# Attention keys loaded once, local scores from row tiles, and weight loads reordered in an attention and mixture-of-experts kernel

## The chip, the core and the metric

The kernel runs on one NeuronCore of a Trainium2 chip. The metric is the device time of one execution in microseconds (us); lower is better. Each engine of the core (TensorE or PE, VectorE or DVE, ScalarE or ACT, GpSimd or POOL, and SyncE or SP, which issues most transfers here) works through its own instructions in a fixed order and waits for the others on semaphores.

## What is computed

Three stages follow each other. The first is attention over 4 batches, 8 heads, 576 positions and 64 channels, the sum of a pooled branch (queries, keys and values averaged over groups of 4 positions) and a local branch (each query sees keys closer than 4 positions):

```
q_d, k_d, v_d = means of q, k, v over 4 neighbouring positions
out_up    = repeat(softmax(scale * q_d @ k_d.T) @ v_d, 4)
mask      = |i - j| < 4
out_local = softmax(where(mask, scale * q @ k.T, -1e9)) @ v
x = out_up + out_local                       # 2304 tokens x 512
```

The second is `h = ((x @ w1) * (x @ w2)) @ w3 @ w_out`, with 64-bit weights that the kernel turns to fp32 itself. The third sends each token to the one expert (of 8) with the largest gate logit: `out = gate * sigmoid(output gate) * relu(h @ w1[e]) @ w2[e]`.

## The kernel before

**Stages.** The kernel first turns the eight pieces of `w_out` from 64-bit to fp32 (`gate_step`, three DVE operations for each piece in `f64_bits`, L127 to L129), then sixteen pieces of `w3` (`w3_part`) and multiplies `w3` with `w_out` on PE (`wc_half`). Behind that come six groups of 384 tokens: `g1_step` (x with w1 and w2) and `g2_step` (with the product of w3 and w_out), both from the helper `mm3` (L398 to L400). Then come the experts. Up to about 104 us of the profiled execution the `w3` stage runs, from there to about 371 us the token groups into which attention is woven, and behind that the experts.

**Attention units.** Attention is cut into 16 units of two heads (`NU`). Each unit has five steps: `a_T` (pooled sums of queries and keys), `a_S1` (scores), `a_S2` (normalizing), `a_V1` (transposes) and `a_V2` (weighted values). The list `side` holds all steps in a staggered order. `step()` takes the next ones out at fixed places of the weight and token loops (tables `GSTEP`, `W3STEP`, `G1STEP`, `G2STEP`), and after a step it issues loads for the next unit. Within that, the framework's list scheduler sets the final order on each engine by its own model of times, so the order of the program text is not that of the engines.

**Keys.** A unit's keys come twice: whole into `kc` (L157, one buffer), which `a_T` sums in fours (`kd`, L185), and head by head into `kz` (L164, one buffer). `kz` has both heads side by side in the free dimension and zeros where a head's row half doesn't belong, so that one matmul with all 128 rows gives both heads' scores. The local scores are 24 fp32 matmuls of 32 queries by 64 columns (two heads of 32 keys), each in one of four 32-column strips of the array:

```python
nc.tensor.matmul(sl[32 * j:32 * j + 32, b], qT[:, 24 * g:24 * g + 32], kz[:, :, 24 * g:24 * g + 32],
                 start=True, stop=True, tile_position=(0, 32 * j))          # L196
```

An fp32 matmul stands in the trace as two records, so a unit has 48 on L196. Three matmuls follow for the pooled scores (`sd`, L208, six records); both groups have the same high priority, and the scheduler may mix them. All their PSUM tiles, and those of `a_V1` and `a_V2`, come from one ring of three banks (`psa`, tag `at`).

**Behind the scores.** DVE adds the mask (L200) and takes the maximum (L201); POOL subtracts it (L202). For the pooled scores DVE takes the maximum (`md`, L211) and scales it (L212), and ACT takes the exponentials with it as bias (L216). POOL adds up pooled values (`v4`, called `v` in the trace, L235 and L236, loaded at L168). The windows of values for the local branch are `vw` (L173).

**Loads.** All these loads, those of the weights (`f64_load`, L119) and the stores of g2_step go through SP's one queue in order. A load whose buffer is still in use makes everything behind it wait. The loads of `w1` and `w2` (`ahead()`) go into other buffers than those of `w3`, and nothing orders the two; `w_gate` and `w_ogate` are loaded in strips of 8 floats (L886, L887).

## Time and profile before

| | us |
|---|---|
| three runs: median (lowest to highest) | 742.13 (741.83 to 745.91) |
| the profiled execution: its own time | 743.41 |
| the profiled execution: span of its instructions | 741.7 |
| PE busy in the span | 706.0 |
| DVE, POOL, ACT busy in the span | 437.9, 324.5, 280.3 |

The mean granted TensorE clock is 0.986 of full speed. Shares of busy time are means over stages that are bound by different things, so the stages have to be looked at one by one: the first 30 us, the rest of the `w3` stage up to 104 us, the token groups with attention up to 371 us, and the experts.

### The profile page before, as it was taken

Reading aid. Unit: us, or ns where it says so; the run is one execution under the profiler, and the core shown is the slowest. Engines: PE = TensorE matmul, PEld = TensorE weight load, DVE = VectorE, ACT = ScalarE, POOL = GpSimd, SP = SyncE. Lnnn points to the kernel's source line nnn. Section 1 sums busy time; section 2 is a strip of 40 time slices with the busy share of each in tenths; the row PEclk is TensorE's granted clock in tenths of the full one; section 3 lists DMA queues with packets and bytes.
Section 4 is the critical chain, followed back from the end, with each engine's and each line's share of the span. In section 5 each row is a group of like instructions: output and inputs, shape, how many; then the busy total and the mean of one; then the engine's idle time right before and its main releaser. Section 6 shows DMA issues by size and latency. Waiting matters only on the chain.

```text
span 741.7 us, 14714 instructions
## 1 busy us (share of the span) xinstructions
PE 706.0 (95%) x5710; PEld 671.9 (91%) x5711; DVE 437.9 (59%) x940; ACT 280.3 (38%) x624; POOL 324.5 (44%) x306
## 2 busy tenths in 40 slices
PE   5788999999999999999999999989999999999995
PEld 3677889989989998998999999979999999999994
DVE  8979899872565437254342342575756756766730
ACT  3436356541254135034212221244454444544610
POOL 6845586950263146123012020155564755854611
PEclk9899999999999999999999999989999999999999
DMA  8998657611153133110100100566444645545301
GB/s 326 316 243 246 186 142 246 212 57 57 28 161 111 43 92 96 57 45 24 57 30 1 43 0 30 171 224 219 170 154 149 218 166 203 184 162 221 115 24 40
DMA packets 38265, 97.72 MB, mean 132 GB/s; under 512 B 6019, under 2 KB 12931, under 8 KB 38193
## 3 DMA queue, kind: packets, MB, share of 16 engines
q1 hardware_dynamic: 34768, 86.82, 36.4%
q0 software_dynamic: 3424, 9.93, 3.7%
q8 instruction: 46, 0.75, 0.4%
q14 instruction: 27, 0.21, 0.1%
HBM read 84.93 MB, written 12.29 MB: 131 GB/s over the span
## 4 chain that ended last, share of the span: by engine, by line
PE 76%; DMA 7%; POOL 6%; issue 6%; DVE 4%; ACT 1%; SPq 0%; POOLq 0%; DVEq 0%; ACTq 0%
PE g L398 22%; PE g L399 21%; PE g L400 21%; DMA v<-in_v_dram 3%; PE at L268 2%; DMA vw<-in_vw_dram 2%; PE at L208 1%; PE at L196 1%; PE tr L694 1%; PE at L264 1%; PE tr L787 1%; PE g L330 1%; PE at L252 1%; POOL out_dram L777 1%; DMA early<-in_moe_w_dram 1%
## 5 line engine op out<-in xcount | busy, mean ns | idle before, releaser
L398 PE MATMUL g<-xh,W 128*128 128x384 f32 x384 | 131.0, 341 | 0.6 <-DVE a L427 0.5
L400 PE MATMUL g<-xh,W 128*128 128x384 f32 x384 | 129.8, 338 | 0.7 <-POOL W L377 0.6
L399 PE MATMUL g<-xl,W 128*128 128x384 f32 x384 | 129.3, 337 | 0.0
L721 DVE TENSOR_TENSOR W<-raw,W 128x1024 fp32r<-128x1024 f32 x32 | 87.9, 2781 | 32.6 <-ACT W L719 23.5
L721 POOL TENSOR_TENSOR W<-raw,W 128x1024 fp32r<-128x1024 f32 x29 | 82.9, 2880 | 36.9 <-ACT W L719 36.9
L398 PE MATMUL g<-xT,W 128*128 128x288 f32 (+6 forms) x256 | 82.0, 320 | 1.0 <-ACT xT L698 1.0
L431 POOL TENSOR_TENSOR h<-a,h 128x384 fp32r<-128x384 f32 x30 | 30.8, 1028 | 118.4 <-ACT h L429 118.4
L399 PE MATMUL g<-xT,W 128*128 128x288 f32 (+6 forms) x256 | 80.1, 313 | 0.0
L400 PE MATMUL g<-xT,W 128*128 128x288 f32 (+6 forms) x256 | 79.8, 312 | 0.0
L398 PEld LDWEIGHTS g<-xh,W 128*128 128x128 f32 x384 | 72.2, 188 | 2.1 <-DVE a L427 0.9
L400 PEld LDWEIGHTS g<-xh,W 128*128 128x128 f32 x384 | 72.1, 188 | 2.0 <-POOL W L377 1.8
L399 PEld LDWEIGHTS g<-xl,W 128*128 128x128 f32 x384 | 72.2, 188 | 0.3 <-issue 0.2
L398 PE MATMUL g<-h,W 128*128 128x288 f32 (+5 forms) x224 | 69.9, 312 | 0.0
L399 PE MATMUL g<-wc,h 128*128 128x272 f32 (+1 forms) x240 | 68.2, 285 | 0.0
L398 PE MATMUL g<-wc,h 128*128 128x272 f32 (+1 forms) x240 | 68.2, 285 | 0.0
L399 PE MATMUL g<-h,W 128*128 128x288 f32 (+5 forms) x224 | 68.0, 303 | 0.0
L400 PE MATMUL g<-h,W 128*128 128x288 f32 (+5 forms) x224 | 68.0, 303 | 0.0
L400 PE MATMUL g<-wc,h 128*128 128x272 f32 (+1 forms) x240 | 67.8, 285 | 0.0
L719 ACT CAST W<-raw 128x1024 fp32r<-128x1024 f32 x61 | 60.0, 1046 | 8.3 <-DMA raw<-in_moe_w_dram 4.4
L427 DVE TENSOR_TENSOR a<-g,a 128x384 f32<-128x384 f32 x48 | 26.6, 554 | 61.9 <-PE g L400 49.6
L747 ACT ACTIVATE h<-g 128x288 fp32r<-128x288 f32 (+6 forms) x64 | 27.9, 437 | 78.1 <-PE g L400 74.2
L777 POOL DMA_INDIRECT out_dram<-orow,b_si x24 | 23.5, 978 | 62.9 <-DVE orow L776 59.3
(255 smaller groups left out, 1716.3 us busy)
## 6 DMA issues: line engine op xcount, KB each, us to landing
raw<-in_moe_w_dram SPq DMA_DIRECT2D x61, 512.0 KB, 3.5
f64w<-in_moe_w_dram SPq DMA_DIRECT2D x16, 512.0 KB, 8.5
f<-in_moe_w_dram SPq DMA_DIRECT2D x16, 512.0 KB, 4.7
vw<-in_vw_dram SPq DMA_DIRECT2D x16, 384.0 KB, 4.9
kc<-in_k_dram SPq DMA_DIRECT2D x16, 288.0 KB, 8.8
qT<-in_q_dram SPq DMA_DIRECT2D x16, 288.0 KB, 3.2
kz<-in_k_dram SPq DMA_DIRECT2D x32, 144.0 KB, 4.1
v<-in_v_dram SPq DMA_DIRECT2D x16, 288.0 KB
```

The source lines that it names most:

```text
L196: nc.tensor.matmul(sl[32 * j:32 * j + 32, b], qT[:, 24 * g:24 * g + 32], kz[:, :, 24 * g:24 * g + 32], start=True, stop=True, tile_positio ...
L208: nc.tensor.matmul(sd[:, qb], qf[:, 96 * qb:96 * qb + 96], d["kd"], start=True, stop=True)
L268: nc.tensor.matmul(xl[c // 3][64 * h:64 * h + 64, 96 * (c % 3):96 * (c % 3) + 96], vw[:, c, D * h:D * h + D], bd[:, 2 * c + h, :], start=T ...
L398: nc.tensor.matmul(ps, whi, xhi, start=first, stop=False)
L399: nc.tensor.matmul(ps, whi, xlo, start=False, stop=False)
L400: return nc.tensor.matmul(ps, wlo, xhi, start=False, stop=last)
L427: nc.vector.tensor_tensor(a, pp[1][:, 0:G], a, op=ALU.mult)
L431: eng.tensor_tensor(lo, a, hi.bitcast(F32), op=ALU.subtract)
L719: nc.scalar.copy(out=hi, in_=t)
L721: ins = eng.tensor_tensor(lo, t, hi.bitcast(F32), op=ALU.subtract)
L747: return nc.scalar.activation(out=t[:, 0, 0:C], in_=ps[:, 0:C], func=AF.Relu), nc.vector.scalar_tensor_tensor(t[:, 1, 0:C], ps[:, 0:C], 0. ...
L777: ins = nc.gpsimd.indirect_dma_start(out=out, out_offset=bass.IndirectOffsetOnAxis(ap=rt["si"][0:n, r, b:b + 1], axis=0), in_=t[0:n], in_o ...
```

## The change

The keys come once, into one of two buffers `kT` (128 rows: both heads' channels). The local scores are 48 matmuls of 32 queries by 32 keys over 64 rows each, head 0 in the upper and head 1 in the lower half of the array's rows, and each head has a PSUM bank of its own. The mask is added per head. The pooled scores are issued behind the local ones (`tc.issue_after`), the scaling of their maximum goes to ACT, the first loads of `w1` and `w2` are issued behind the last load of `w3`, and the two gate matrices are laid out by the host so that each row is one piece of 128 bytes.

```diff
@@ -101,6 +101,7 @@
 
 
     staged = {}
+    f64_last = [None]
 
     def pieces(m, n):
         return (slice(0, 256), slice(256, 512)) if (m, n) == ("o", 0) else (slice(0, 512),)
@@ -116,7 +117,7 @@
             t = mt([P, 512], I64, "f64", tag=f"W{3 + 4 * m}") if n % 2 and n < 6 else mt([P, 512], I64, "f64", bufs=2)
             src = (w1, w2)[m][n]
         for c in pieces(m, n):
-            nc.sync.dma_start(out=t[:, c], in_=src[:, c])
+            f64_last[0] = nc.sync.dma_start(out=t[:, c], in_=src[:, c])
         staged[m, n] = t
 
     def f64_bits(t, dst):
@@ -138,11 +139,11 @@
     def at(shape, dt, name, bufs=1):
         return att.tile(shape, dt, name=name, tag=name, bufs=bufs)
 
-    kz = at([P, 2, 584], F32, "kz")
+    kTs = [at([P, 584], F32, f"kT{i}") for i in range(2)]
     qTs = [at([P, 584], F32, f"qT{i}") for i in range(2)]
     bd = at([P, 12, 96], F32, "bd")
     qz = at([P, 2, 144], F32, "qz")
-    for t in (kz, *qTs, bd, qz):
+    for t in (*qTs, *kTs, bd, qz):
         nc.gpsimd.memset(t, 0.0)
     st = {}
 
@@ -152,16 +153,10 @@
 
     def a_load(u):
         d = st.setdefault(u, {})
-        qT = qTs[u % 2]
-        kc = at([P, S], F32, "kc")
-        nc.sync.dma_start(out=kc, in_=k[u])
+        qT, kT = qTs[u % 2], kTs[u % 2]
+        nc.sync.dma_start(out=kT[:, 3:3 + S], in_=k[u])
         nc.sync.dma_start(out=qT[:, 0:S], in_=q[u])
-        d.update(kc=kc, qT=qT)
-
-    def a_loadk(u):
-        for h in range(2):
-            c = slice(64 * h, 64 * h + 64)
-            nc.sync.dma_start(out=kz[c, h, 3:3 + S], in_=k[u, c])
+        d.update(kT=kT, qT=qT)
 
     def a_loadd(u):
         v4 = at([72, 2, 4, 2 * D], F32, "v4")
@@ -182,34 +177,37 @@
             c = slice(64 * h, 64 * h + 64)
             nc.gpsimd.tensor_tensor(qz[c, h], hs[c, :, 0], hs[c, :, 1], op=ALU.add)
         dn = at([P, 144], F32, "kd")
-        nc.vector.tensor_reduce(out=dn, in_=d["kc"].rearrange("p (n t) -> p n t", t=4), axis=AX.X, op=ALU.add)
+        nc.vector.tensor_reduce(out=dn, in_=d["kT"][:, 3:3 + S].rearrange("p (n t) -> p n t", t=4), axis=AX.X, op=ALU.add)
         d["kd"] = dn
 
     def a_S1(u):
         d = st[u]
-        qT = d["qT"]
-        ps = psa.tile([P, 512], F32, name="at", tag="at")
-        sl = ps[:, 0:384].rearrange("p (b h k) -> p b h k", b=6, h=2)
+        qT, kT = d["qT"], d["kT"]
+
+        sl = [psa.tile([P, 512], F32, name="at", tag="at")[:, 0:192].rearrange("p (b k) -> p b k", b=6) for _ in range(2)]
         with burst():
             for g in range(24):
                 b, j = divmod(g, 4)
-                nc.tensor.matmul(sl[32 * j:32 * j + 32, b], qT[:, 24 * g:24 * g + 32], kz[:, :, 24 * g:24 * g + 32],
-                                 start=True, stop=True, tile_position=(0, 32 * j))
+                for h in range(2):
+                    c = slice(64 * h, 64 * h + 64)
+                    end = nc.tensor.matmul(sl[h][32 * j:32 * j + 32, b], qT[c, 24 * g:24 * g + 32], kT[c, 24 * g:24 * g + 32],
+                                     start=True, stop=True, tile_position=(64 * h, 32 * j))
         sm = at([P, 6, 2, 32], F32, "sm", bufs=2)
         mx = at([P, 6, 2], F32, "mx")
-        nc.vector.tensor_tensor(sm, sl, mask.unsqueeze(2).to_broadcast([P, 6, 2, 32]), op=ALU.add)
+        for h in range(2):
+            nc.vector.tensor_tensor(sm[:, :, h], sl[h], mask, op=ALU.add)
         nc.vector.tensor_reduce(out=mx, in_=sm, axis=AX.X, op=ALU.max)
         nc.gpsimd.tensor_tensor(sm, sm, mx.unsqueeze(3).to_broadcast([P, 6, 2, 32]), op=ALU.subtract)
         ps = psa.tile([P, 512], F32, name="at", tag="at")
         sd = ps[0:96, 0:432].rearrange("p (q k) -> p q k", q=3)
         qf = qz.rearrange("p h n -> p (h n)")
-        with burst():
+        with burst(), tc.issue_after(end.ins):
             for qb in range(3):
                 nc.tensor.matmul(sd[:, qb], qf[:, 96 * qb:96 * qb + 96], d["kd"], start=True, stop=True)
         ed = at([96, 3, 144], F32, "ed", bufs=2)
         md = at([96, 3], F32, "md")
         nc.vector.tensor_reduce(out=md, in_=sd, axis=AX.X, op=ALU.max)
-        nc.vector.tensor_scalar(md, md, -1.0 / 128, None, op0=ALU.mult)
+        nc.scalar.mul(md, md, -1.0 / 128)
         zd = at([96, 3], F32, "zd", bufs=2)
         nc.scalar.activation(out=sm, in_=sm, func=AF.Exp, scale=0.125)
         for qb in range(3):
@@ -303,8 +301,6 @@
                 if fn is a_T and u + 1 < NU:
                     a_load(u + 1)
                 if fn is a_S1:
-                    if u + 1 < NU:
-                        a_loadk(u + 1)
                     a_loadd(u)
 
 
@@ -883,14 +879,13 @@
     nc.vector.memset(wg, 0.0)
     for n in range(KF):
         if n == 1:
-            nc.sync.dma_start(out=wg[:, :, 0:E], in_=w_gate.rearrange("(k p) e -> p k e", p=P))
-            nc.sync.dma_start(out=wg[:, :, E:2 * E], in_=w_ogate.rearrange("(k p) e -> p k e", p=P))
+            nc.sync.dma_start(out=wg[:, :, 0:E], in_=w_gate.rearrange("p (k e) -> p k e", e=E))
+            nc.sync.dma_start(out=wg[:, :, E:2 * E], in_=w_ogate.rearrange("p (k e) -> p k e", e=E))
         f64_load("o", n)
     for n in range(4):
         f64_load("3", n)
         if n == 1:
             a_load(0)
-            a_loadk(0)
     gps = ps2.tile([P, 512], F32, name="g2", tag="g2")
     for f in range(KF):
         gate_step(f, gps, staged.pop(("o", f)))
@@ -913,7 +908,8 @@
     wf3 = mt([P, 3, 512], F32, "wf3", tag="xl")
     for i in range(KF):
         if i == KF - 2:
-            ahead()
+            with tc.issue_after(f64_last[0].ins):
+                ahead()
         w3T[i] = [mt([P, KF, P], F32R, "w3T", tag=f"W{12 + 2 * (i % 2) + z}") for z in range(2)]
         for hf in range(2):
             n = 2 * i + hf
@@ -1072,6 +1068,8 @@
     a["moe_w3"] = w3.reshape(KF, P, 2, 4, P).transpose(0, 2, 4, 3, 1).reshape(2 * KF, P, 512)
     for n in ("moe_w1", "moe_w2"):
         a[n] = _np.asarray(a[n]).reshape(KD, P, KF, P).transpose(2, 1, 0, 3).reshape(KF, P, 512)
+    for n in ("moe2_w_gate", "moe2_w_output_gate"):
+        a[n] = _np.asarray(a[n]).reshape(KD, P, E).transpose(1, 0, 2).reshape(P, KD * E)
     w = _np.asarray(a["moe2_w1"])
     a["moe2_w1"] = w.reshape(E, KD, P, 4, 256).transpose(0, 3, 2, 1, 4).reshape(E, 4 * P, 1024)
     w = _np.asarray(a["moe2_w2"])
```

**On SP's queue**, from the loads of the first attention unit on. Before (`f64w` is a piece of `w3`, `f_` one of `w1` or `w2`, `v_` the pooled values):

```order
L119 DMA f64w<-in_moe_w_dram 128x512 x2
L158 DMA qT_113<-in_q_dram 128x576
L168 DMA v_380<-in_v_dram 72x1024
L173 DMA vw<-in_vw_dram 128x768
L119 DMA f_1138<-in_moe_w_dram 128x512
L119 DMA f_1140<-in_moe_w_dram 128x512
L119 DMA f_1142<-in_moe_w_dram 128x512
L157 DMA kc<-in_k_dram 128x576
L164 DMA kz<-in_k_dram 64x576 x2
L158 DMA qT_112<-in_q_dram 128x576
L119 DMA f_1144<-in_moe_w_dram 128x512
L119 DMA f64w<-in_moe_w_dram 128x512 x2
```

Of the change:

```order
L120 DMA f64w<-in_moe_w_dram 128x512 x2
L157 DMA kT_112<-in_k_dram 128x576
L158 DMA qT_114<-in_q_dram 128x576
L163 DMA v_402<-in_v_dram 72x1024
L168 DMA vw<-in_vw_dram 128x768
L157 DMA kT_111<-in_k_dram 128x576
L158 DMA qT_113<-in_q_dram 128x576
L120 DMA f64w<-in_moe_w_dram 128x512 x2
```

The four `f_` loads that stood between those of `w3` now stand behind the last of `w3` (twelve of its pieces came after them), and the keys of a unit are one row in place of three.

**On PE**, at the scores of the last attention unit (L196 and L208 before, L193 and L206 now; `g_` is the work of the token groups, L264 the next step of another unit). Before:

```order
L400 MATMUL g_4431<-xh,W_1619 128x384
L196 MATMUL at<-kz,qT_113 32x64 x3
L208 MATMUL at<-kd,qz 96x144
L196 MATMUL at<-kz,qT_113 32x64
L208 MATMUL at<-kd,qz 96x144
L196 MATMUL at<-kz,qT_113 32x64
L208 MATMUL at<-kd,qz 96x144
L196 MATMUL at<-kz,qT_113 32x64 x19
L264 MATMUL at<-pt,vd 64x144 x4
```

Of the change:

```order
L395 MATMUL g_4801<-xl,W_1731 128x384
L396 MATMUL g_4801<-xh,W_1732 128x384
L193 MATMUL at<-kT_112,qT_114 32x32 x48
L206 MATMUL at<-kd,qz 96x144 x3
L394 MATMUL g_4816<-xh,W_1742 128x384
```

The pooled matmuls no longer stand among the local ones, whose number has doubled.

**On PE, at one of six units** in which the two heads now stand apart (L266 is the last step of another unit):

```order
L266 MATMUL at<-bd,vw 64x96 x12
L193 MATMUL at<-kT_111,qT_113 32x32 x24
L394 MATMUL g_3820<-xh,W_1742 128x384
L395 MATMUL g_3820<-xl,W_1742 128x384
L193 MATMUL at<-kT_111,qT_113 32x32 x24
L206 MATMUL at<-kd,qz 96x144 x3
L193 MATMUL at<-kT_112,qT_114 32x32 x48
```

There the first 24 matmuls are those of one head and the second 24 those of the other, with other work between them; behind them the next unit's scores follow at once.

## Rows read from the trace of the kernel before

**Rows 1.** The page's busy time of each engine, its share of the span and instructions.

```profile
PE 706.0 (95%) x5710; PEld 671.9 (91%) x5711; DVE 437.9 (59%) x940; ACT 280.3 (38%) x624; POOL 324.5 (44%) x306
```

**Rows 2.** Busy time by stage: PE, PEld, DVE, ACT, POOL, granted clock, DMA, GB/s.

```profile
0.00:30.00 30.00, 18.35 (x153) 13.32 (x154) 25.86 (x58) 12.61 (x27) 20.93 (x42) 1.00 0.95 327
30.00:104.00 74.00, 65.17 (x738) 58.54 (x739) 65.07 (x141) 33.30 (x96) 44.57 (x52) 0.93 0.77 215
104.00:371.00 267.00, 264.56 (x2392) 249.48 (x2391) 148.99 (x398) 101.55 (x271) 106.99 (x120) 1.00 0.31 94
```

**Rows 3.** What PE waited for from 30 to 104 us: total us, times, longest.

```profile
PE g L398 <- DVE wc L363: 2.3, 1, 2.3
PE g L400 <- POOL w3T L351: 2.2, 1, 2.2
```

**Rows 4.** Two shorter stretches, PE alone: busy, granted clock, DMA, GB/s.

```profile
31.50:38.40 6.90, 5.47 (x30) 0.51 1.04 316
75.90:79.30 3.40, 3.40 (x25) 0.50 0.03 7
```

**Rows 5.** What DVE waited for from 30 to 104 us.

```profile
DVE kd L185 <- DMA kc<-in_k_dram: 3.8, 2, 2.4
DVE sT L243 <- POOL sm L228: 2.6, 1, 2.6
```

**Rows 6.** What POOL waited for from 30 to 104 us.

```profile
POOL v L235 <- DMA v<-in_v_dram: 18.6, 6, 5.3
```

**Rows 7.** What SP's queue waited for from 30 to 104 us.

```profile
SPq L119 <- DVE wf L129: 20.2, 9, 6.0
...
SPq L164 <- PE at L196: 4.2, 2, 3.1
```

**Rows 8.** The page's DMA issues: count, KB each, median us from issue to landing.

```profile
raw<-in_moe_w_dram SPq DMA_DIRECT2D x61, 512.0 KB, 3.5
f64w<-in_moe_w_dram SPq DMA_DIRECT2D x16, 512.0 KB, 8.5
...
kz<-in_k_dram SPq DMA_DIRECT2D x32, 144.0 KB, 4.1
```

**Rows 9.** The first three loads of w1 and w2 on SP's queue: start, us.

```profile
20.45 1.52 SPq L119 DMA_DIRECT2D f<-in_moe_w_dram  x3
```

**Rows 10.** PE at the last unit's scores, in order of time: start, us to the last end.

```profile
337.57 0.31 PE L196 MATMUL at<-kz,qT 128*32 128x64 f32 x6
337.81 0.49 PE L208 MATMUL at<-kd,qz 128*96 128x144 f32 x2
338.23 0.30 PE L196 MATMUL at<-kz,qT 128*32 128x64 f32 x2
...
340.21 0.47 PE L264 MATMUL at<-pt,vd 72*64 72x144 f32 x4
```

**Rows 11.** PE at the scores of a unit that wasn't mixed.

```profile
287.92 0.88 PE L196 MATMUL at<-kz,qT 128*32 128x64 f32 x48
288.72 0.98 PE L208 MATMUL at<-kd,qz 128*96 128x144 f32 x6
289.44 0.43 PE L398 MATMUL g<-xh,W 128*128 128x384 f32 x1
```

**Rows 12.** PE at the first local scores: two windows, of one and of four records.

```profile
22.43 0.24 PE L196 MATMUL at<-kz,qT 128*32 128x64 f32 x1
...
22.43 0.26 PE L196 MATMUL at<-kz,qT 128*32 128x64 f32 x4
```

**Rows 13.** Groups of operations on DVE, 30 to 371 us: busy us, mean ns, idle before.

```profile
L200 DVE TENSOR_TENSOR sm<-at,mask 128x384 f32<-128x384 f32 x15 | 8.1, 540 | 0.2
L212 DVE TENSOR_SCALAR md<-md 96x3 f32<-96x3 f32 x15 | 6.2, 416 | 0.0
```

**Rows 14.** Groups of operations on ACT, the whole span.

```profile
L216 ACT ACTIVATE ed<-at,md 96x144 f32<-96x144 f32 x48 | 17.5, 371 | 20.7 <-DVE md L212 20.6
...
L271 ACT COPY up<-at 128x144 f32<-128x144 f32 x16 | 4.4, 278 | 19.8 <-PE at L268 19.3 <-ACT sm L214 0.2
```

## The prediction

> **What bounds the kernel now.** I first read the page's busy times [rows 1]: PE works 706.0 of 741.7 us, so the end is set by PE wherever PE is full, and by whoever starves it elsewhere. The table by stage tells where that is [rows 2]. From 104 to 371 us PE works 264.56 of 267.00 us at the full clock: there every microsecond of PE work that goes comes off the end, and faster transfers are worth next to nothing. From 30 to 104 us PE and DVE both work 65.1 of 74.0 us, the DMA engines are 0.77 busy, and the clock is 0.93. Before 30 us DVE works 25.86 of 30.00 us and PE 18.35. The experts behind 371 us keep their order and aren't touched.
>
> For the stage from 30 to 104 us I then read the waits. PE's own are single stalls of 2.3 and 2.2 us for DVE and POOL results [rows 3], and in two stretches of 6.90 and 3.40 us its clock is at half, 1.2 in place of 2.4 GHz [rows 4]; both follow stalls of PE. DVE stood 3.8 us for the keys' load and 2.6 us for a POOL product [rows 5]. POOL, which works in order, stood 18.6 us for the pooled values' loads [rows 6]. SP's queue mostly waits for DVE to free a weight buffer (20.2 us), but also 4.2 us for the local scores, before it may overwrite the one `kz` buffer [rows 7]. A 512 KB load takes 8.5 us to land in this stage and 3.5 us in the experts' stage [rows 8]. So this stage is a loop of DVE, POOL and late transfers; its floor, if nothing waits, is DVE's 65.1 us.
>
> **The change part by part. Transfers in the w3 stage.** The 32 loads of `kz`, 144 KB each [rows 8], go: 4.6 MB in all, about 0.3 MB a unit. Three of the four early loads of w1 and w2 start at 20.45 us [rows 9], ahead of most of w3; all four, 2 MB, now come behind w3, where the order shows them. With about five units in the stage some 3.5 MB leaves the crowded stretch, and at 215 GB/s [rows 2] that is 16 us of transfer time, none of it itself on the path. What shrinks is what DVE waits for: the 3.8 us for keys should go whole, since `kT` has two buffers and its load now stands before that of the values, and of the 2.6 us behind POOL I take half, 1.2, since POOL's loads come sooner but still through single buffers. That makes 5.0 us. The ends: all of DVE's idle time, 74.0 less 65.07, 8.9 us gained; or nothing, with a new stall of the size seen there, 2.3 us [rows 3], lost, because the scheduler's order is new in the whole stage. I take 5.0, nearest to the rows that name a transfer. If the cover fails and the moved loads come too late for the first token group, one landing of 8.5 us [rows 8] is the price; DVE has to turn the last w3 piece before it can touch them, so I cost the move at nothing.
>
> **Pooled scores behind the local ones.** In the last unit the three pooled matmuls stand apart among the local ones, and the unit's scores take 340.21 - 337.57 = 2.64 us of PE [rows 10]. In a unit that isn't mixed they take 289.44 - 287.92 = 1.52 us [rows 11]. Three returns from pooled to local matmuls thus cost 1.12 us, 0.37 each. Behind 104 us the order had 14 such returns in ten units; now none is left inside a unit. That gives 14 x 0.37 = 5.2 us on the path. Against it three of the nine units that remain there have their heads apart, with other work between. I price such an extra entry like a return, 0.37 us, so 1.1 us is lost; the ends are nothing and three times a return's pair of switches, 2.2 us. Net: 4.1 us gained. In the w3 stage the order loses five more returns, 1.9 us, which I count at nothing, since DVE sets the pace there; if DVE's waits go, it is the cover.
>
> **Row tiles.** A unit now has 96 records of half the columns, where it had 48. Today 48 take 288.72 - 287.92 = 0.80 us, 16.7 ns each with the entry [rows 11]. If the two row halves ran side by side at no cost of issue, half the columns on twice the tiles would take half, 0.40 us. If each record held PE as long as one does now, 96 would take 1.60 us. Four records that start on four free strips end 0.02 us after the first alone would (0.26 against 0.24) [rows 12], so about 6.7 ns apart. That is the nearest row for what issue allows: 96 x 6.7 ns is 0.64 us, and with the entry (0.80 less 47 x 14 ns, 0.14 us) 0.78, as good as today's. I take zero. The ends over nine units are 3.6 us gained and 7.2 us lost.
>
> The Trainium skill has a rule that speaks against this: TensorEngine Tiling (Array Packing), Instruction Overhead, says that each matmul carries about 60 cycles, so that no tiling factor should come from a dimension that is already small, and 32 columns are under 60. Read as a cost of each record in turn, that is 25 ns at 2.4 GHz, my estimate from that page, 96 of them 2.4 us a unit, and the sum would be 14 us worse. The trace does not bear that reading out: 48 records in 0.80 us are 16.7 ns each [rows 11].
>
> **Mask, scaling, gates.** DVE's one mask addition of 540 ns becomes two of half the elements, 540 together or at most 1080; the scaling on DVE, 416 ns in the mean, goes [rows 13]. On DVE that is 0.4 us less to 0.1 us more a unit, and DVE works 148.99 of 267.00 us behind 104 us [rows 2], so it hides there. ACT gets a small operation, at most the 278 ns of its copy of 144 columns; it stood 20.6 us waiting for the scaled maximum [rows 14], so it has the room. The gates' loads lie in the first 5 us beside DVE's work of 25.86 of 30 us. I count all three at nothing.
>
> **The sum.** The profiled execution took 743.4 us: 741.7 of span and 1.7 around it. 743.4 - 5.0 - 4.1 + 0 = 734.3. The median of the runs, 742.1, lies 1.3 lower, inside their spread of 741.8 to 745.9, so I give 734.
>
> **The rivals.** *DVE keeps its pace in the w3 stage.* The saved waits come back at another place, such as SP's 20.2 us for freed weight buffers [rows 7], which no lighter traffic shortens. For it: DVE is 88% busy there. Against it: two of its waits name a transfer or what hangs on one. Time: 743.4 - 4.1 = 739.3.
>
> *Records are issued one after another.* If 96 records in two row halves hold PE as long each as 48 do now, the nine units lose 7.2 us: 734.3 + 7.2 = 741.5. For it: no row shows more than four strips at work. Against it: the 6.7 ns [rows 12].
>
> *The ring of three banks* is the one on the slow side. A unit's scores now hold all three `at` banks: two until the mask is added, the third until ACT has read it three times. PE's order is fixed, so the next transposes, and every matmul of the token groups behind them, stand until DVE or ACT lets go. The third bank is held for at least the scaling and three exponentials, 278 + 3 x 371 ns, 1.4 us [rows 14]. If PE stands for all of it in nine units, 12.6 us are lost: 734.3 + 12.6 = 746.9. It makes the kernel slower by more than can be told apart once a unit loses over (745.8 - 734.3) / 9 = 1.3 us. Against it: PE has other work in its order behind most scores, and no wait for a bank stands among the two largest today [rows 3].
>
> *All gains at their ends:* 743.4 - 8.9 - 5.2 - 3.6 = 725.7.
>
> **How the numbers follow.** A measurement of this kernel can tell about 0.5% from no change: under 738.4 us is faster, over 745.8 slower. The forecast, 734, has a chance of 0.49; all gains, 726, 0.06; DVE's pace, 739, 0.17, half on either side of 738.4; issue, 741.5, 0.15; the ring, 747, 0.10; and 0.03 stays for the serial reading of the 60 cycles (the row of 16.7 ns against it), on the slow side too. Faster: 0.49 + 0.06 + 0.08 = 0.63. Same: 0.09 + 0.15 = 0.24. Slower: 0.13. The range runs from all gains to just above the issue rival, 726 to 743, and leaves out the ring and little else.
>
> **What would show it.** Right: from 30 to 104 us, stretched to where the first token group now begins, that beginning comes about 5 us sooner, with DVE's wait for keys gone and pooled values landing faster; behind it the last group's attention ends about 9 us sooner than 371; a unit's scores take about 1.5 us on PE, with 96 records in some 0.8 us. Wrong: DVE as idle as before, 96 records in 1.6 us, or PE waiting at scores and transposes for DVE's mask or ACT's exponentials by a microsecond a unit.

## The result and the profile after

| | median of the runs, us | lowest to highest |
|---|---|---|
| before | 742.28 | 739.4 to 747.76 |
| changed | 747.34 | 744.72 to 752.82 |

The changed kernel takes 1.0066 times as long, with a 95% interval of 1.0048 to 1.0084: slower by 0.66%, just past the 0.5% that the prediction called measurable. The forecast was 734. The profiled execution took 748.93 us, with a span of 747.1 and a mean granted clock of 0.979 (before: 0.986).

The page, busy time and an instruction queue (queue, packets, MB, share of the DMA engines); I take it for PE's, since it had 46 packets before and grew with PE's instructions:

```profile
PE 707.3 (95%) x6478; PEld 677.1 (91%) x6479; DVE 442.9 (59%) x940; ACT 281.6 (38%) x640; POOL 324.6 (43%) x307
...
q8 instruction: 52, 0.85, 0.5%
```

PE has 768 records more than in [rows 1] and is busy 1.3 us longer. Part of that is the clock, since a record lasts longer at a lower one. My estimate takes the span times what the mean granted clock lacks to 1 off the busy time: 706.0 - 741.7 x 0.014 = 695.6 us before, 707.3 - 747.1 x 0.021 = 691.6 now. Counted at full speed, then, some 4 us of work did go off PE.

The same stages as in [rows 2]:

```profile
0.00:30.00 30.00, 17.75 (x281) 12.88 (x283) 26.33 (x58) 12.55 (x27) 21.89 (x45) 0.99 0.85 299
30.00:104.00 74.00, 68.22 (x1024) 61.96 (x1024) 72.74 (x156) 37.28 (x115) 46.86 (x56) 0.94 0.69 209
104.00:371.00 267.00, 258.17 (x2700) 246.56 (x2699) 146.51 (x381) 99.28 (x267) 103.08 (x114) 0.98 0.26 80
```

From 30 to 104 us DVE is now busy 72.74 of 74.00 us, where it was 65.07: its idle time did go, as forecast, and yet the stage didn't end sooner (the first token group begins at 105.7 us; before, at 105.2). Most of that time didn't become useful work. One operation on 96x3 numbers, here before and in the change (busy us, mean ns), lasts far longer; why is open:

```profile
L229 DVE TENSOR_SCALAR zd<-zd 96x3 f32<-96x3 f32 x4 | 1.2, 290 | 0.9 <-ACT ed L216 0.9
```

```profile
L227 DVE TENSOR_SCALAR zd<-zd 96x3 f32<-96x3 f32 x6 | 7.1, 1180 | 0.0
```

It makes up 5.9 of DVE's 7.7 us more. Behind 104 us PE, which had 2.4 us of idle time, now has 8.8, and a clock of 0.98 in place of 1.00. There the loss shows.

What DVE and POOL waited for from 30 to 104 us, beside [rows 5] and [rows 6]:

```profile
POOL v L233 <- DMA v<-in_v_dram: 14.7, 6, 4.4
...
DVE kd L180 <- DMA kT<-in_k_dram: 0.7, 1, 0.7
```

DVE's 3.8 us for keys shrank to 0.7 and its wait for POOL is gone. The four moved loads of w1 and w2, three of which were issued at 20.45 us [rows 9], now stand here in SP's queue (start, us, count), and two key loads behind them took 14.85 us to leave it, since a key buffer comes free only with an earlier unit's sums and scores:

```profile
78.95 1.76 SPq L120 DMA_DIRECT2D f<-in_moe_w_dram  x4
...
84.29 14.85 SPq L157 DMA_DIRECT2D kT<-in_k_dram  x2
```

PE's waits from 20 to 300 us (us in total, times, longest):

```profile
PE g L394 <- DVE wc L359: 4.9, 4, 3.4
PE at L193 <- issue: 2.9, 2, 1.6
PE at L193 <- ACT pt L251: 2.1, 1, 2.1
...
PE at L193 <- DVE sm L198: 1.4, 1, 1.4
```

L193 is the local scores. Before, PE stood 1.0 us at the local scores in the whole execution, once, for a key load; now it stood 6.4 us in the middle of score blocks, twice for nothing that the profile shows ("issue"), and twice for something that looks like a PSUM bank of the ring: the weights' copy (`pt`) and the mask's sum (`sm`) release banks. That it was a bank is read from the names, not shown.

### The profile page after: what moved, and what is told of

Same layout as the page of the kernel before. It is cut to its first block, busy times and chain, and to the rows that moved or that the text cites. A ratio compares the mean times of both kernels' runs of the same rounds, so it can differ in the third digit from the quotient of the medians.

```text
span 747.1 us, 16194 instructions
## 1 busy us (share of the span) xinstructions
PE 707.3 (95%) x6478; PEld 677.1 (91%) x6479; DVE 442.9 (59%) x940; ACT 281.6 (38%) x640; POOL 324.6 (43%) x307
## 4 chain that ended last, share of the span: by engine, by line
PE 73%; DVE 8%; DMA 7%; issue 6%; POOL 4%; ACT 1%; SPq 0%; POOLq 0%; DVEq 0%
PE g L394 22%; PE g L396 22%; PE g L395 21%; DMA v<-in_v_dram 2%; PE at L193 2%; DMA f64w<-in_moe_w_dram 1%; DVE cv L129 1%; DVE cv L128 1%; PE tr L690 1%; PE at L266 1%; DMA vw<-in_vw_dram 1%; DVE wf L130 1%; PE tr L783 1%; PE at L206 1%; POOL W L373 1%
## 5 line engine op out<-in xcount | busy, mean ns | idle before, releaser
L394 PE MATMUL g<-xh,W 128*128 128x384 f32 x384 | 131.2, 342 | 2.1 <-ACT W L372 1.4
L394 PE MATMUL g<-xT,W 128*128 128x288 f32 (+6 forms) x256 | 81.6, 319 | 1.0 <-ACT xT L694 1.0
L394 PEld LDWEIGHTS g<-xh,W 128*128 128x128 f32 x384 | 72.8, 189 | 3.4 <-ACT W L372 1.7
L394 PE MATMUL g<-h,W 128*128 128x288 f32 (+5 forms) x224 | 69.9, 312 | 0.0
L394 PE MATMUL g<-wc,h 128*128 128x272 f32 (+1 forms) x240 | 68.3, 285 | 0.0
```

Of the source, the lines that this page charges most:

```text
L394: nc.tensor.matmul(ps, whi, xhi, start=first, stop=False)
```

## The experiments

All ratios are to the kernel before, measured on the same chip. "24" and "48" are the matmuls in a unit's local scores.

| kernel | scores | ratio [95% interval] |
|---|---|---|
| e3: before, local scores in two banks | 24, two banks | 0.9998 [0.9977, 1.0020] |
| i3: before, w1 behind w3 | 24 | 1.0019 [0.9997, 1.0040] |
| e4: before, pooled behind local | 24 | 0.9937 [0.9914, 0.9961] |
| f4: e4, two banks | 24, two banks | 0.9948 [0.9927, 0.9968] |
| i2: e4, w1 behind w3 | 24 | 0.9941 [0.9919, 0.9964] |
| j2: i2, gates laid out | 24 | 0.9914 [0.9879, 0.9949] |
| j1: i2, scaling on ScalarE | 24 | 0.9883 [0.9856, 0.9911] |
| f2: e4, gates and scaling | 24 | 0.9958 [0.9935, 0.9982] |
| f3: i2, gates and scaling | 24 | **0.9844 [0.9815, 0.9873]** |
| i1: f3, two banks | 24, two banks | 0.9944 [0.9922, 0.9966] |
| i4: f3, head by head, one bank | 48, full array | 1.0102 [1.0077, 1.0127] |
| h1: f3, head by head, two banks | 48, full array, two banks | 1.0021 [0.9998, 1.0044] |
| h2: f3, row tiles (keys twice) | 48, rows, two banks | 1.0007 [0.9981, 1.0034] |
| f5: e4, row tiles (keys twice) | 48, rows, two banks | 1.0121 [1.0084, 1.0158] |
| **the change** | 48, rows, two banks | 1.0066 [1.0048, 1.0084] |
| e1: the change, w1 free | 48, rows, two banks | 1.0034 [1.0011, 1.0058] |
| e2: the change, pooled free | 48, rows, two banks | 1.0115 [1.0074, 1.0156] |

**Which part loses: first four kernels.** Each undoes or does one thing.

```diff
 e1, of the change:
-            with tc.issue_after(f64_last[0].ins):
-                ahead()
+            ahead()
 e2, of the change:
-        with burst(), tc.issue_after(end.ins):
+        with burst():
 e4, of the kernel before: the line of e2 the other way round
 e3, of the kernel before:
-                nc.tensor.matmul(sl[32 * j:32 * j + 32, b], ...
+                nc.tensor.matmul(sl[b // 3][32 * j:32 * j + 32, b % 3], ...
```

> The changed kernel with w1's loads no longer held behind the last load of w3. Order theory (the change put the attention ahead of the w1 and w2 loads in the w3 stage, and the engines then stand idle between 104 and 170 us): w1's and w2's first tiles land earlier, the idle time of VectorE in 104 to 165 us goes from some 9 us back towards 4, and the kernel takes 741 to 744 us. Bank theory (the local scores take two of the three PSUM banks of the ring, and TensorE stands in the middle of the score block): nothing changes, 746.5 to 748 us, and the four stops of 1.3 to 2.1 us at the scores stay.

> The changed kernel with the pooled scores free to go before the local ones. The forecast's own term: without that order TensorE returns to its row-tiled and back to full mode 14 more times at 0.37 us, less what splitting cost, so some 4 us slower than the change, 751 us. Bank theory: with the pooled scores first, all three banks are still asked for, so the stops stay, 747 us or more. Order theory: the pooled scores' place decides little, 746 to 749 us.

> The kernel before, its matmuls as they are, but with the local scores written to two PSUM banks (blocks 0 to 2 and 3 to 5) and so two mask adds of half the size in place of one. Bank theory: the ring of three is short as in the changed kernel, TensorE stands some 1.3 us at several score blocks, 746 to 749 us. Order theory: only the second add's fixed part is paid, 742 to 744 us.

> The kernel before with one thing of the change: the pooled scores wait for the local ones. The forecast's term: 14 returns of 0.37 us fewer in the attention, 738 to 740 us if TensorE's order sets the time there, and 742 us if what TensorE saves is given back to waits. Order theory and bank theory both leave the kernel at 742 us or under it, since this touches neither the loads nor the number of banks.

The pooled scores' place is worth what was forecast, from both sides: 0.63% gained on the kernel before (e4), 0.49% lost when it is undone in the change (e2), that is 4.7 and 3.6 us; the forecast said 4.1, or 5.2 without the heads set apart, as in e4. The last unit in e4, beside [rows 10], in order of time:

```profile
335.07 0.88 PE L196 MATMUL at<-kz,qT 128*32 128x64 f32 x48
335.88 0.98 PE L208 MATMUL at<-kd,qz 128*96 128x144 f32 x6
336.78 0.47 PE L264 MATMUL at<-pt,vd 72*64 72x144 f32 x4
```

The unit takes 336.78 - 335.07 = 1.71 us in place of 2.64. w1's place costs the change 0.3% (e1; the two intervals overlap), less than the order theory asked for. Two banks cost the kernel before nothing (e3), which speaks against the bank theory. So the loss lay elsewhere, and the row tiles were left.

**All but the row tiles, and the row tiles alone.**

```diff
 f5 (of e4) and h2 (of f3), rows from the zero-padded keys, two banks, two mask sums:
-                end = nc.tensor.matmul(sl[32 * j:32 * j + 32, b], qT[:, 24 * g:24 * g + 32], kz[:, :, 24 * g:24 * g + 32],
-                                 start=True, stop=True, tile_position=(0, 32 * j))
+                for h in range(2):
+                    c = slice(64 * h, 64 * h + 64)
+                    nc.tensor.matmul(sl[h][32 * j:32 * j + 32, b], qT[c, 24 * g:24 * g + 32], kz[c, h, 24 * g:24 * g + 32],
+                                     start=True, stop=True, tile_position=(64 * h, 32 * j))
 f2 (of e4): the change's two hunks on the gates, and
-        nc.vector.tensor_scalar(md, md, -1.0 / 128, None, op0=ALU.mult)
+        nc.scalar.mul(md, md, -1.0 / 128)
 f3 (of f2): the change's hunk on ahead()
```

> The kernel before with three parts of the change: pooled scores behind the local ones, gates laid out, ScalarE scaling the pooled maximum. Left out: the row tiles with the keys loaded once, and w1's loads behind w3's. Forecast's terms (0 for gates and scale): as the pooled scores behind alone, which ran at 0.994 of the kernel before, 737 to 739 us. If gates or the moved scaling are what reorders the work in the w3 stage: 741 us or more.

> All of the change but the row tiles and the keys loaded once: that is, the kernel before it with w1's loads held behind w3's added. If w1's place costs by itself (the changed kernel without it ran at 1.0034 against 1.0066): some 2.4 us slower than without, 740 to 742 us. If w1's place costs only because the attention has been pulled ahead by the single key load: 737 to 739 us. If the rows are innocent and the rest is what loses: 745 us or more.

> The kernel before with the pooled scores behind the local ones, and the local scores (full array, as they were) written to two banks of the ring with two mask adds. Pooled scores behind alone ran at 0.994, two banks alone at 1.000. Bank theory (two banks and then a third in one fixed order stop TensorE in the middle of the block): 742 us or more, with stops over 1 us at the scores. Rows theory (records and the clock that goes with their stops, not the banks): 738 to 740 us.

> The kernel before with the local scores as row tiles that read the zero-padded keys as they were loaded before (both key loads stay), and the pooled scores behind them; loads, gates and scaling as before. Records theory (8.7 ns a record in place of 6.7 ns: 0.15 us for a unit, 0.3 us for one cut in two, by 16): 2.5 to 4 us over the pooled scores behind alone, 741 to 742 us. Bank theory: some 4 us more by stops at four score blocks, 744 to 746 us. Order theory (the single key load is what pulls the attention ahead and loses the time): 738 to 740 us.

f3, the change without row tiles and single key load, takes 732.14 us in the median and beats both kernels. f5, row tiles alone on e4, takes 753.25, 13.7 us more than e4 by the ratios and well above every figure expected of it. f4 is within the interval of e4: in this order two banks cost nothing either.

**Rows, banks or the number of matmuls.** h1 has the change's number of matmuls and its banks, but each matmul over all 128 rows; h2 the same with rows. i1 and i4 take banks and number apart.

```diff
 h1, of h2:
-   ... qT[c, 24 * g:24 * g + 32], kz[c, h, 24 * g:24 * g + 32], ... tile_position=(64 * h, 32 * j))
+   ... qT[:, 24 * g:24 * g + 32], kz[:, h, 24 * g:24 * g + 32], ... tile_position=(0, 32 * j))
 i4, of h1: one bank and one mask sum, as before
-   ... sl[h][32 * j:32 * j + 32, b], ...
+   ... sl[32 * j:32 * j + 32, b, h], ...
 i1, of f3: the edit of e3
```

> The kernel with all of the change but the row tiles and the single key load (732 us), and in it the local scores head by head: 48 matmuls for a unit in place of 24, alternating between two PSUM banks as the row tiles do, but each over all 128 rows with the zero-padded keys. So it has the row tiles' records, banks, two adds and instruction count, without row tiles. Records and instruction-supply theory (twice the matmuls in one block: stops at the second of two neighbouring score blocks, 2.5 us after TensorE's instruction queue began a 16 KB transfer, and the lower clock behind them): 742 to 748 us. Row-mode theory (half of the array is what costs, by more time for a record and by the clock): 733 to 737 us.

> The changed kernel with the keys loaded twice as before, the row tiles reading the halves of the zero-padded tile. If the single key load costs by pulling the attention ahead: 735 to 742 us. If the row tiles' score block itself costs, whatever the loads: 744 to 750 us, as the changed kernel or above.

> The kernel with all of the change but the row tiles and the single key load (0.984 of the kernel before), its 24 matmuls of the local scores written to two banks (blocks 0 to 2 and 3 to 5) with two mask adds. Bank theory: most of what the row tiles lost comes with the second bank, 742 to 746 us. Number theory (48 matmuls in place of 24): 732 to 735 us, as two banks cost 0.1% on the kernel with the pooled scores behind alone.

> The same kernel (0.984 of the kernel before) with its local scores head by head, 48 matmuls over the full array in place of 24, all in one bank, one mask add. Number theory: 740 to 746 us, most of what the row tiles lost. Bank theory: 733 to 737 us (only the records' own time, 0.15 us for each of 16 units).

h1 and h2 can't be told apart, so row mode as such makes no difference beyond their intervals, some 0.25% to either side. i4 differs from f3 in one thing, 48 matmuls in place of 24, and loses 2.6%, 19 us. i1 loses 1.0%, but e3 and f4 lost nothing by the same edit, and h1, with a second bank, is faster than i4: the bank has no constant price. Where both sides have two banks, 48 cost less: 0.8% (h1 against i1) and 1.7% (f5 against f4). Over all kernels with the pooled scores behind, the eight with 24 matmuls lie from 0.9844 to 0.9958 (mean 0.9921), the six with 48 from 1.0007 to 1.0121 (mean 1.0059). They don't overlap; the means differ by 1.4%, 10 us. So the number of matmuls costs time; where, the profiles tell in part.

One stretch goes from where PE first works at the router's token table (L538 before) to where the token groups' last `xh` record starts. It holds eight of the 16 units, and PE works nearly all of it. Before, e4, i4 and h1 (length, PE busy):

```profile
193.50:453.50 260.00, 259.06 (x2166) 248.57 (x2165) 118.28 (x361) 82.64 (x219) 70.17 (x83) 1.00 0.18 56
```

```profile
194.20:449.50 255.30, 254.53 (x2167) 247.05 (x2167) 118.84 (x361) 81.95 (x219) 69.58 (x83) 1.00 0.19 57
```

```profile
206.30:463.60 257.30, 256.90 (x2551) 249.88 (x2550) 116.74 (x353) 83.07 (x227) 70.32 (x83) 1.00 0.19 57
```

```profile
193.20:451.40 258.20, 257.56 (x2552) 249.74 (x2551) 116.51 (x361) 83.47 (x227) 70.39 (x83) 1.00 0.19 56
```

With 24 matmuls and the pooled scores free (before, e3, i3) it takes 258.2 to 260.1 us, with 24 and pooled behind (eight kernels) 254.4 to 255.3, with 48 and pooled behind (six) 257.3 to 260.1. Here both prices stand clear in every kernel: the pooled order saves 4.7 us in the mean, 48 matmuls cost 4.0. (e2 takes 259.0, no more than the change with its 259.5, so e2's loss lies elsewhere and confirms the pooled order only in its total.) The stretch ahead of it holds the rest of the 10 us, 5.6 in the mean, but there the two groups overlap, 190.0 to 196.8 against 193.2 to 206.3, and each edit also gives another order. That part of the price is not traced to the matmuls.

**A fourth bank.** The conversions' scratch `cv` gives its bank to the ring and moves to SBUF; h3 is the change with it, h4 is f3 with it.

```diff
-    psa = actx.enter_context(tc.tile_pool(name="psa", bufs=3, space=PSUM))
+    psa = actx.enter_context(tc.tile_pool(name="psa", bufs=4, space=PSUM))
-        c = psc.tile([P, 512], F32, name="cv", tag="cv")...
+        c = att.tile([P, 512], F32, name="cv", tag="cv")...
```

> The changed kernel with a fourth bank in the ring of the attention's PSUM tiles; the conversions' scratch, which had that bank, lies in SBUF. Bank theory: the waits inside the score blocks for a bank (2.1 us behind the copy of the weights, 1.4 us behind the sum of the mask) go, and with them the lower clock behind them: 739 to 743 us. Instruction-supply and records theories: 745 to 748 us.

> Control for the fourth bank: the kernel with all of the change but the row tiles and the single key load (732 us), with the same fourth bank and scratch in SBUF. All theories: within 3 us of 732 us; what it differs by is the price of the scratch in SBUF and of the fourth bank without row tiles, to be taken from the other.

Both ran far off: 1.0299 [1.0265, 1.0334] and 1.0275 [1.0242, 1.0308]. DVE's conversions of the w1 and w2 pieces in h4 (mean ns behind the busy time):

```profile
L128 DVE SCALAR_TENSOR_TENSOR cv<-f,cv 128x512 uint32<-128x512 uint32 x16 | 20.2, 1264 | 0.4
...
L129 DVE SCALAR_TENSOR_TENSOR wf<-f,cv 128x512 uint32<-128x512 uint32 x16 | 15.4, 960 | 0.6
```

Before, with the scratch in PSUM, the same lines took 688 and 683 ns. From 30 to 104 us DVE is busy 72.57 of 74.00 us in h4, 64.94 in f3. The slower conversions probably set the start and hide what a bank is worth, so this pair decides nothing about banks.

**Where f3's gain comes from.** i2 and i3 have the two orders alone, j1 and j2 add one of the parts forecast at nothing.

> The kernel before with two parts of the change: pooled scores behind the local ones and w1's loads behind w3's. If the gain of the kernel with all but the row tiles comes from these two: 731 to 734 us. If it needed the gates' layout or ScalarE's scaling, or is an accident of one order: 736 to 740 us.

> The kernel before with w1's loads behind w3's alone. If that is worth by itself what it was worth beside the pooled scores (0.9844 against 0.9958, some 8 us): 734 to 737 us. If its worth hangs on the rest of the order, as with the row tiles, where it cost 0.3%: 740 to 745 us.

> The kernel before with pooled scores behind the local ones, w1's loads behind w3's (these two: 0.9941) and ScalarE scaling the pooled maximum. If the scaling on ScalarE is what takes these two to 0.984 (16 instructions of 0.4 us off VectorE, which is nearly full in the w3 stage): 731 to 734 us. If it is the gates' layout or one lucky order: 737 to 741 us.

> The kernel before with pooled scores behind the local ones, w1's loads behind w3's (these two: 0.9941) and the gates laid out. If the gates' layout (the first loads end sooner) is what takes these two to 0.984: 731 to 734 us. If it is the scaling on ScalarE or one lucky order: 737 to 741 us.

w1's place is worth nothing alone (i3) and nothing beside the pooled scores (i2 against e4), but 1.1% when gates and scaling are there (f3 against f2). Gates and scaling lose 0.2%, inside both intervals, without it (f2 against e4) and gain 1.0% with it (f3 against i2), the scaling 0.6% by itself (j1); the gates alone (j2) can't be told from i2. Such terms don't add. From e4 to f3 these six kernels lie within 0.9 us of each other in the stretch shown above, so most of what they gain or lose lies ahead of it, in the first 190 us, where each edit gives the scheduler another order. Whether f3 is more than the best of several orders stays open.

## Why the prediction failed

**The row tiles, counted at zero, are the step that failed.** Put on f3 they cost 1.6% (h2), put on e4 1.8% (f5). Three things stand in the traces of kernels that have them; the forecast had priced only the first, and its sum had no term for the clock.

*The records' own time.* A unit on PE in the change, in f3 and in i4 (start, us to the last end, count):

```profile
220.05 1.02 PE L193 MATMUL at<-kT,qT 64*32 64x32 f32 x96
221.00 0.98 PE L206 MATMUL at<-kd,qz 128*96 128x144 f32 x6
```

```profile
218.06 0.88 PE L197 MATMUL at<-kz,qT 128*32 128x64 f32 x48
218.87 0.98 PE L209 MATMUL at<-kd,qz 128*96 128x144 f32 x6
```

```profile
235.20 1.17 PE L198 MATMUL at<-kz,qT 128*32 128x32 f32 x96
236.30 0.98 PE L210 MATMUL at<-kd,qz 128*96 128x144 f32 x6
```

From the first local record to the first pooled one it takes 0.95, 0.81 and 1.10 us. The 96 row-tile records are 8.7 ns apart by their starts, not the 6.7 that the prediction took from four records [rows 12]; over the full array 96 of half the width are 10.2 ns apart. Four records that find all strips free don't show what a block does: in the change, too, the first four start 7 ns apart, and the fifth 33 ns behind the fourth. The prediction's own 14 ns for a whole block of 48 was the nearer row. So two row halves side by side save a little against one after the other, but not what the doubled number costs. In 16 units the 0.145 us that row tiles take longer are 2.3 us, and a unit cut in two takes twice 0.56. This lies well inside the prediction's bounds of 3.6 us gained and 7.2 lost.

The Trainium skill's advice in TensorEngine Tiling (Array Packing), Instruction Overhead, that no tiling factor should come from a dimension that is already small, came out right here. Splitting 64 columns into twice 32 cost time in every pair of kernels compared above, 0.8 to 2.6%. The rival that the prediction made of it, some 25 ns for each record, did not: the trace shows 8.7.

*The supply of instructions.* The wait called "issue" in the change, in order of time (idle before and releaser in brackets):

```profile
277.12 0.62 PE L193 MATMUL at<-kT,qT 64*32 64x32 f32 x48
277.68 0.98 PE L206 MATMUL at<-kd,qz 128*96 128x144 f32 x6
278.58 0.82 PE L193 MATMUL at<-kT,qT 64*32 64x32 f32 x73
281.00 0.33 PE L193 MATMUL at<-kT,qT 64*32 64x32 f32 x23 [1.59 <-issue]
```

PE stops after 73 of a unit's 96 records, right behind the second half of another unit. In the 1.1 us from 278.5 the DMA view shows one packet of an instruction queue among the other traffic:

```profile
q8 instruction: 1, 0.02, 5.5%
```

It starts at 278.53 us, in a DMA share of 0.94 to 0.96, and PE goes on 2.47 us later. (From the packet to the end of the stop the share was 0.58 to 1.02 in the five cases told here, so a full DMA isn't needed.) The other such stop, at 27.75 us, ends 2.50 us after a packet of that queue began. In e1 the two stops of the kind end 2.59 and 2.43 us after one, and i4 has one in its pooled scores, 2.78 us after one. Here is the one behind 270 us in e1, and the one of i4:

```profile
PE at L193 <- issue: 1.6, 1, 1.6
```

```profile
PE at L210 <- issue: 1.3, 1, 1.3
```

No kernel with 24 matmuls has an "issue" stop over 0.6 us from 20 to 480 us; the queue moves 46 packets of 16 KB in each of these and 52 in each with 48. I read it as two dense score blocks using up PE's instructions faster than the next 16 KB arrive. That is argued from the timing in five places, not shown by an experiment. The Trainium skill (Runtime: NRT & Kernel Launch, Instruction fetch mechanics) says that instructions are refilled in blocks of 16 KiB and that crossing a boundary is mostly hidden. The packet size agrees with the trace; if my reading is right, hidden it was not here, at 1.3 to 1.65 us a time. Of the seven kernels with 48 matmuls in the table only the change, e1 and i4 have such stops (h2 has one of 0.7 us, h1, f5 and e2 have none), so they are a part of the loss at most.

*The clock.* PE around the stop at 281 us (busy by engine, granted clock, DMA share, GB/s):

```profile
278.54:279.40 0.86, 0.86 (x74) 0.73 (x74) 0.86 (x3) 0.07 (x1) 0.77 (x2) 1.00 0.94 267
279.40:281.00 1.60, 0.01 (x1) 0.00 (x0) 0.56 (x1) 1.32 (x7) 0.07 (x1) 1.00 0.96 262
281.00:281.70 0.70, 0.70 (x25) 0.66 (x25) 0.26 (x1) 0.00 (x0) 0.35 (x1) 1.00 0.84 316
281.70:285.10 3.40, 3.40 (x12) 3.40 (x12) 2.27 (x7) 0.53 (x2) 3.40 (x5) 0.50 0.59 182
285.10:288.50 3.40, 3.40 (x22) 3.39 (x22) 2.37 (x6) 1.78 (x5) 3.19 (x5) 1.00 0.00 0
```

After 1.60 us of standing still PE runs 3.40 us at 1.2 GHz and issues 12 records, where it issues 22 in the next 3.40 us. So the stop costs 1.6 and the clock another 1.7, which with the records' 0.145 us in eight units accounts for most of the 5.1 us that the change loses to f3 in the stretch from 199.9 us on (below). In the first 480 us the change has five stretches at half the clock (29.1 to 32.5, 39.4 to 42.8, 83.7 to 87.1, 111.0 to 117.9, 281.7 to 285.1 us), each beginning within a stop of PE or at most 1.6 us behind one. Two of these stops are the "issue" stops or stand just behind one, two are those that look like a bank, and the longest stretch, 6.9 us, belongs to a stop of 3.4 us for a product of w3 and w_out, which is not at the scores at all. f3 has one stretch, from 80.1 us, within a stop of 3.4 us. A stop alone doesn't decide: this one of 1.99 us in f3 left the clock at full:

```profile
28.53:30.52 1.99, 0.00 (x1) 0.00 (x0) 1.08 (x2) 1.37 (x8) 1.84 (x4) 1.00 0.84 302
30.52:34.00 3.48, 3.13 (x65) 2.80 (x66) 3.48 (x12) 0.62 (x1) 2.59 (x4) 1.00 0.63 158
```

Why the change's shorter stops were enough is open; row mode alone doesn't explain the loss, since h1 and h2 take the same time.

**The account.** Three stretches, cut where PE first works at the router's token table and where the token groups' last `xh` record starts. First of the kernel before, whose middle one stands above:

```profile
0.00:193.50 193.50, 171.50 (x1629) 154.95 (x1631) 153.14 (x343) 83.30 (x213) 114.54 (x142) 0.97 0.64 195
...
453.50:741.70 288.20, 275.45 (x1919) 268.43 (x1917) 166.43 (x237) 114.33 (x192) 139.82 (x81) 0.98 0.45 158
```

Then of the change and of f3:

```profile
0.00:199.90 199.90, 174.65 (x2013) 158.98 (x2015) 161.35 (x343) 83.81 (x221) 113.93 (x143) 0.96 0.55 176
199.90:459.40 259.50, 257.91 (x2551) 250.50 (x2550) 115.39 (x361) 83.77 (x227) 70.41 (x83) 0.99 0.16 48
459.40:747.10 287.70, 274.74 (x1918) 267.60 (x1916) 166.17 (x237) 114.01 (x192) 140.27 (x81) 0.98 0.46 158
```

```profile
0.00:190.00 190.00, 164.55 (x1628) 150.51 (x1630) 149.48 (x334) 85.27 (x221) 113.84 (x142) 0.99 0.63 199
190.00:444.40 254.40, 254.40 (x2168) 247.23 (x2167) 118.15 (x353) 83.60 (x227) 70.67 (x83) 1.00 0.19 57
444.40:732.90 288.50, 275.10 (x1918) 267.90 (x1917) 166.23 (x237) 114.02 (x192) 139.83 (x81) 0.98 0.46 157
```

Against the kernel before, the forecast had 5.0 us off the first stretch and most of its 4.1 off the second. The change takes 6.4 us more in the first and 0.5 less in each of the others. By cause, PE's idle time (length less busy) grew by 4.1 us (39.8 against 35.7), what the clock takes by 5.3 (15.7 against 10.4), and PE's work at full speed fell by 4.0. So the waits, forecast to shrink by 5.0, grew, and the clock, without a term in the sum, took as much again.

Against f3 the change loses 9.9 us in the first stretch and 5.1 in the second, and wins 0.8 back in the third: 14.2. By cause: PE's idle time is 39.8 against 38.9 us, 0.9 more. The clock takes the span times what the mean granted clock lacks to 1: 747.1 x 0.021 = 15.7 us against 732.9 x 0.010 = 7.3 (f3's is 0.990), 8.4 more. What is left, 4.9 us, is PE's work counted at full speed: the scores' 2.3 us from above, the units cut in two, and other returns between tile shapes. So the clock is the largest item between these two, ahead of the records themselves. These are single executions, but the clock of all runs agrees: 0.981 in the mean for the change and 0.991 for f3, which by the same estimate is 14.1 against 6.6 us. It is not so for 48 matmuls in general: h1 (0.986) and h2 (0.985) owe the clock 3.5 and 4.6 us more than f3 but are some 13 and 12 us slower, and f5 (0.981) owes it 3.7 more than e4 (0.985) of its 13.7. The first stretch still holds 25 us of idle time in both kernels; there another order, not only another duration, may have moved the waits about, and the runs don't separate the two.

**The transfers in the w3 stage, forecast at 5.0 us gained, gave nothing.** The waits named did shrink (keys 3.8 to 0.7 us, pooled values 18.6 to 14.7), but w1's place by itself is worth nothing (i3, i2), and the single key load rather loses: the change stands 0.6% above h2. Attention ran ahead in that stage and the weights fell behind: the third unit's output was ready at 71.4 in place of 80.3 us, the last piece of w1 and w2 at 167.7 in place of 161.3, and at 111.55 us PE had stood 3.4 us, the longest stretch at half the clock beginning in it, until a product of w3 and w_out was taken out of its bank (`wc`, the wait on L394 above). "DVE keeps its pace", a rival with 0.17, was right that this term brings nothing.

**Pooled behind local, forecast at 4.1, gave 3.6 to 4.7.** Right in size, and in mechanism where e4 shows it: the middle stretch falls from 260.0 to 255.3 us.

**Mask, scaling, gates, counted at nothing:** right on the kernel with pooled behind alone (f2), wrong beside w1's place (j1, j2, f3), where they bring up to 1%. That f3 comes out at 732, next to the forecast of 734, is therefore no proof of the forecast's sum: the 5 us that it put on the transfers came only from edits in company.

**The rivals.** "Records are issued one after another" asked for 1.6 us a unit; it was 0.95. "The ring of three banks" gave 746.9, next to the result, and two of the stops inside the blocks (2.1 and 1.4 us) carry its mark. That its number fits is luck, for it can't be the main cause: with one bank and 48 matmuls i4 loses more than the change, and with two banks and 24 matmuls e3 and f4 lose nothing. A share of it stays possible, since i1 lost 1.0% by the second bank.

## What to carry to other kernels

Count what a finer tiling does to the number of matmuls before counting what it saves in columns: here 24 small matmuls becoming 48 cost 0.8 to 2.6% by the pair compared, whether as row tiles or over the full array, and records were only part of it. Price a stall on a full TensorE with the clock that may follow it: here one of 1.6 us cost 3.3, though one of 1.99 us in f3 cost no clock. And when a change has six parts, run it without its riskiest one; f3, the change without row tiles and single key load, is 1.6% faster than the kernel before.

## What the runs showed of the hardware

- TensorE stood five times for 1.3 to 1.65 us in or right behind dense blocks of 32-column matmuls with nothing in the profile to wait for, each time until 2.4 to 2.8 us after a 16 KB packet of an instruction queue began. That it ran short of instructions is the likely reading, not a tested one.
- Two row tiles of 64 rows each are issued 8.7 ns apart, full-array matmuls of the same 32 columns 10.2 ns, those of 64 columns 14.0 ns on average in a block.
- DVE's 128x512 conversions of the w1 and w2 pieces took 877 to 1264 ns with their scratch in SBUF (h4), 683 to 689 with it in PSUM (before); h4, which differs from f3 by that and the fourth bank, takes 4.4% longer.
